# Long-convolution stage: all 16 tap units with two ScalarE products and two partial sums, first output rows and residual addition inside the fixed order, fixed order made anew

## Chip, cores, metric

The kernel runs on one core of a Trainium2 chip. The metric is the device time of one execution in microseconds. Times inside the profile are counted from the start of the profiled execution's span. The engines are TensorE (PE; PEld is its weight load), VectorE (DVE), ScalarE (ACT), GpSimd (POOL) and SyncE (SP), which issues most DMAs. Each engine runs its own instructions in order; between engines they wait on semaphores.

## What is computed

One adaLN block on S = 2048 rows of D = 448 channels, float32, batch 1. Cut to what matters:

```python
sa, ca, ga, sb, cb, gb = (silu(c) @ w_mod) in six pieces of D
h  = layernorm(x) * (1 + ca) + sa                   # x = A_q
# conv branch: short causal conv of K, times V, long causal conv, gate
k_shift = sum(k_pad[:, t:t + S, :] * shift_k[:, 3 - t] for t in range(4))
kv = k_shift * v
y  = irfft(rfft(kv, 2 * S) * rfft(ssm_k, 2 * S))[:S] + kv * ssm_D
x  = x + ga * (h * y)
# gated MLP, F = 1792
h  = layernorm(x) * (1 + cb) + sb
x  = x + gb * ((sigmoid(h @ w_gate) * (h @ w_up)) @ w_down)
```

## The kernel before, in words

There are two parts. The second, the gated MLP, is a long run of TensorE matmuls from about 169 us to the end. The first is the conv branch, and only this one is changed.

**Conv branch.** The channels are handled in two halves `h` of C = 224, and each half in two groups `c` of DT = 112. The long convolution is done as a discrete Fourier transform in matrix form, in steps, for the filter (`k`, tile `ak`) and for the signal (`v`, tile `av`): `s1k`/`s1v` (TensorE, first transform; four indices `i` with two halves `e` each), `e1k`/`e1v` (ScalarE copies the result from PSUM, L262), `tk`/`tv` (VectorE transposes in place a block `n` of eight, L212), `s2k`/`s2v` (TensorE, second transform, L277 and L329), `ek` (ScalarE copy, L280). Then per block the complex product: `m0` and `m1` (VectorE, L332 and L335; `m1` reads a copy `kx` with exchanged parts, which SP's DMAs make, L249), `sa` (TensorE, back transform, L342), `st` (VectorE transpose from PSUM, L346). When the blocks of a half are done, `stage_out` makes output rows `y` (TensorE, L361) from the transposed blocks; `y` of the second half is split for its first four row tiles into `y10`: the columns of blocks 0 to 6 (196 of 224), and those of block 7 (28).

**Taps.** The short convolution works on k stored with the channels on partitions: a unit is (h, i, c), 16 in all, each 112x512. A unit has four taps `t0` to `t3`: a product (`product`, L295 ScalarE or L297 GpSimd) writes into one of six accumulators, and `add_tap` (VectorE, L302, a fused multiply-add) adds a tap to a partial sum: its last argument says which. Tap 3 is written in place over the k tile. Units of half 0 have one product (GpSimd) and three additions into one sum; units of half 1 have one product on GpSimd and one on ScalarE, and one addition to each, thus two partial sums. `kv` (TensorE, L310) turns a unit by transposes against the identity and adds up the partial sums in PSUM: four matmuls for one sum, eight for two. `vm` (VectorE, L314) multiplies by v.

**Beside it.** The layer norm's sums of a row tile pair `ln` (ScalarE, L440 and L441), square root `sq` (ScalarE, L445), its end `le` (VectorE reciprocal and product, L449 and L450), normalised rows `gn` (ScalarE for half 1, L457; GpSimd for half 0, L459), modulation `gm` (GpSimd, two instructions, L463 and L464), the gate's products and sums `ga` and `gb` (GpSimd). The modulation vectors come from `wm` (load), `part` (TensorE), `pc` (ScalarE), `sum` (TensorE), `sc`. 

**What sets the order.** All of this stands in one table, `ORDER`, a list of items that is run from left to right (`run`). An item `t1.1.0.0.a.4` is tap 1 of unit (1, 0, 0) as a product on ScalarE into accumulator 4 (`p`: GpSimd, `d`: VectorE's addition to the sum numbered last); `kv.0.3.0:1` has behind the colon its PSUM buffer (0 to 3: t0, t1, sa, y). Each engine executes its part of the list in that order and nothing is reordered afterwards. SP's loads, too, are issued in the order of the list. Behind `run(ORDER)` follow, in written code, the first weight forms (`plain_hi`, ScalarE), the two pieces of `y10` (`stage_out`), their gate (VectorE, L618: `gg = gg * y`, both pieces), the addition into `x1` (L621), and the statistics of the second layer norm (`ln2_stats`, L476).

Of the kernel before, what the change touches and what calls it, by code (L numbers as in the profile page):

```python
# [32 lines left out]
kv.0.3.1 s2k.0.0:3 tk.0.3 e1v.0.2.1 wm.1 s2k.0.2:0 vm.0.1 ek.0.0 s1k.1.3.1:3 vm.0.3 ek.0.2 s1v.0.1.1:2 t2.1.1.0.d.0 e1k.1.3.1 da.1 s1v.0.3.0:1 tk.0.4
e1v.0.1.1 t0.1.3.1.p.5 s1v.0.1.0:3 t3.1.1.0.d.1 e1v.0.3.0 t2.1.3.1.d.0 s1v.0.3.1:2 t0.1.2.1.p.4 e1v.0.1.0 tk.0.1 s2k.0.4:1 e1v.0.3.1 t2.1.2.1.d.0
s2k.0.1:3 ek.0.4 tv.0.6 s1k.1.0.0:2 ek.0.1 t2.1.0.1.d.0 s1k.1.2.1:1 e1k.1.0.0 tk.0.5 s2k.0.3:3 e1k.1.2.1 s1k.1.1.0:2 t3.1.0.1.d.1 ek.0.3 tv.0.4
kv.1.0.0:1 t0.1.1.1.p.0 e1k.1.1.0 s2k.0.5:3 tk.0.6 t1.1.1.1.a.3 kv.1.0.1 ek.0.5 t2.1.1.1.d.0 s1k.1.0.1:2 tv.0.2 t1.1.2.1.a.1 s2k.0.6:3 e1k.1.0.1
t3.1.2.1.d.1 s1k.1.3.0:0 t3.1.1.1.d.1 ek.0.6 s1k.1.1.1:2 tv.0.0 e1k.1.3.0 kv.1.1.0:3 tk.0.7 e1k.1.1.1 s1k.1.2.0:0 t1.1.3.1.a.2 tv.0.7 kv.1.1.1
e1k.1.2.0 t3.1.3.1.d.1 s2k.0.7:2 ln.0 vm.1.1 vm.1.0 s1v.1.1.1:3 t0.1.2.0.p.2 s1v.1.1.0:0 tk.1.5 t0.1.3.0.p.0 ek.0.7 s1v.1.0.0:1 t2.1.2.0.d.0
t1.1.2.0.a.3 t2.1.3.0.d.0 s1v.1.0.1:2 e1v.1.1.1 t3.1.2.0.d.1 e1v.1.1.0 part.1:3 tk.1.7 t1.1.3.0.a.3 kv.1.2.0:0 tk.1.1 wm.0 pc.1 e1v.1.0.1 kv.1.2.1
t3.1.3.0.d.1 e1v.1.0.0 tk.1.3 kv.1.3.0:2 ln.1 sum.1 vm.1.2 kv.1.3.1 tk.1.2 s1v.1.2.1:0 kx.0.0:0 vm.1.3 s1v.1.2.0:1 e1v.1.2.1 tk.1.0 s1v.1.3.0:2  # L40
# [71 lines left out]
def adaln_conv_glu_kernel(ctx: ExitStack, tc: tile.TileContext, q, kT, v, ssm, shift, dskip,  # L112
# [503 lines left out]
    for c, y in zip(parts, y10):  # L616
        gg = four(gt[1, 0], c)
        DVE.tensor_mul(gg, gg, y.rearrange("p b (j c) -> p b j c", c=C)[:, :, :, c])  # L618
# [614 lines left out]
```

## Time and profile before

| what | value |
|---|---|
| timed runs, median of 3 | 553.51 us (553.46 to 553.8) |
| profiled execution, its own time | 553.13 us |
| its span, first to last instruction | 551.3 us |
| PE busy | 526.7 us (96%) |
| VectorE busy | 445.9 us (81%) |
| ScalarE busy | 259.1 us (47%) |
| GpSimd busy | 84.5 us (15%) |
| mean granted TensorE clock | 0.99 |

The shares are means over two parts with different limits, so they do not say which engine the conv branch waits for; tables of stretches, waits and single rows do. In rows of the timeline the first number is the start and the second the duration, in us; what stands in square brackets is the idle time of the engine ahead of the row, and who ended it. Successive instructions of an engine overlap a little, so the distance of two starts is what one takes of its queue.

### The profile page before, as it was taken

The numbers are of one execution on the slowest core, as the hardware profiler recorded it, in microseconds if no ns is written. First come the engines' busy times: TensorE is split into PE (matmuls) and PEld (weight loads), VectorE is DVE, ScalarE is ACT, GpSimd is POOL, SyncE is SP. The second block draws the span as 40 slices with busy tenths as digits, with TensorE's granted clock in tenths as the row PEclk, the third lists the DMA queues.
The fourth block names the chain that finished last, engine by engine and source line by source line (L and its number), as shares of the span: only waits on it lengthen the run. The fifth ranks groups of instructions, "written<-read, shape, count | busy, mean of one in ns | idle before, by whom it ended". The sixth has DMA issues, their size and how long they took to land.

```text
span 551.3 us, 7602 instructions
## 1 busy us (share of the span) xinstructions
PE 526.7 (96%) x2886; PEld 414.6 (75%) x2886; DVE 445.9 (81%) x551; ACT 259.1 (47%) x444; POOL 84.5 (15%) x64
## 2 busy tenths in 40 slices
PE   3799999999799999999999999999999999999997
PEld 3676733343578888888888888888888888888886
DVE  4999999998898878898998988884646466969565
ACT  1389999821676585375455543421212122424120
POOL 5742216999200000000000000000000000000000
PEclk9799999999899999999999999999999999999999
DMA  8995487872030429486966394767464661220103
GB/s 304 391 410 213 123 247 191 239 200 60 1 111 0 168 92 347 158 324 223 355 243 256 125 360 139 264 229 251 126 210 124 219 226 62 85 98 15 53 0 134
DMA packets 28600, 101.66 MB, mean 184 GB/s; under 512 B 4242, under 2 KB 4756, under 8 KB 27540
## 3 DMA queue, kind: packets, MB, share of 16 engines
q1 hardware_dynamic: 21828, 76.12, 42.1%
q10 hardware_dynamic: 6736, 25.06, 11.6%
q8 instruction: 23, 0.38, 0.3%
q14 instruction: 13, 0.11, 0.1%
HBM read 64.86 MB, written 28.44 MB: 169 GB/s over the span
## 4 chain that ended last, share of the span: by engine, by line
PE 75%; DVE 10%; ACT 5%; DMA 4%; issue 3%; SPq 2%; POOL 0%; DVEq 0%; ACTq 0%
PE d L793 24%; PE b L759 16%; PE c L759 10%; PE a L759 10%; PE gu L881 5%; PE s1k L257 2%; DMA kTa<-in_wmod_dram 2%; SPq L249 1%; PE sa L342 1%; PE kv L310 1%; PE y L361 1%; PE s1v L257 1%; DVE spare L302 1%; PE s2k L277 1%; ACT gbrow L441 1%
## 5 line engine op out<-in xcount | busy, mean ns | idle before, releaser
L793 PE MATMUL d<-wd,h 128*128 128x448 f32 x666 | 144.4, 366 | 0.2
L793 PEld LDWEIGHTS d<-wd,h 128*128 128x128 f32 x666 | 124.7, 188 | 13.1 <-DVE wd L513 1.0
L759 PE MATMUL b<-xt,ring 128*128 128x512 f32 x408 | 99.0, 391 | 0.0
L759 PEld LDWEIGHTS b<-xt,ring 128*128 128x128 f32 x408 | 76.5, 188 | 14.9 <-ACT wd L509 0.2
L808 DVE TENSOR_TENSOR x<-x,d 128x896 f32<-128x896 f32 x55 | 59.5, 1083 | 16.6 <-PE d L793 16.5
L759 PE MATMUL a<-x,ring 128*128 128x512 f32 x264 | 63.8, 389 | 0.0
L759 PEld LDWEIGHTS a<-x,ring 128*128 128x128 f32 x264 | 49.6, 188 | 10.2
L768 ACT ACTIVATE h<-st 128x512 fp32r<-128x512 f32 x55 | 34.6, 629 | 31.4 <-DVE st L777 19.0
L771 DVE TENSOR_TENSOR h<-st,h 128x512 fp32r<-128x512 f32 x55 | 37.8, 688 | 12.5 <-ACT h L768 12.2
L774 ACT ACTIVATE st<-st 128x512 f32<-128x512 f32 x24 | 15.2, 632 | 63.8 <-DVE st L1117 36.0
L881 PE MATMUL gu<-x,ring 128*128 128x512 f32 x176 | 42.7, 397 | 0.0
L1071 ACT ACTIVATE st<-st 128x512 f32<-128x512 f32 x12 | 7.6, 631 | 68.0 <-DVE st L1070 68.0
L881 PEld LDWEIGHTS gu<-x,ring 128*128 128x128 f32 x176 | 33.4, 192 | 7.0 <-DVE inb L922 0.3
L759 PE MATMUL c<-x,ring 128*128 128x512 f32 x144 | 34.8, 390 | 0.0
L740 ACT ACTIVATE ring<-sum 128x512 fp32r<-128x512 f32 x28 | 17.2, 625 | 31.7 <-DVE sum L721 16.8
L759 PEld LDWEIGHTS c<-x,ring 128*128 128x128 f32 x144 | 27.0, 188 | 5.2
L342 PE MATMUL sa<-m,wa 128*64 128x448 f32 x128 | 27.1, 548 | 2.4 <-DVE m L335 2.4
L759 PE MATMUL c<-xt,ring 128*128 128x512 f32 x120 | 29.2, 389 | 0.0
L777 DVE TENSOR_TENSOR st<-st 128x512 f32<-128x512 f32 x24 | 16.6, 691 | 11.9 <-ACT st L774 11.7
L759 PEld LDWEIGHTS c<-xt,ring 128*128 128x128 f32 x120 | 22.5, 188 | 4.6
L342 PEld LDWEIGHTS sa<-m,wa 128*64 128x64 f32 x128 | 8.4, 136 | 20.1 <-issue 12.1
L262 ACT ACTIVATE ak<-s1k 128x896 f32<-128x896 f32 x16 | 14.4, 920 | 19.0 <-PE s1k L257 19.0
(189 smaller groups left out, 830.1 us busy)
## 6 DMA issues: line engine op xcount, KB each, us to landing
fd<-ring ACTq DMA_DIRECT2D x35, 512.0 KB, 5.2
...
```

The costliest lines, as they stand in the source:

```text
L257: PE.matmul(y, zc[r, g + jj], xs_[r, jj], start=True, stop=True)
L262: ACT.activation(d, y, AF.Copy)
L342: PE.matmul(wide[r, b, :, :56], wa[:, b, r], pairs2(ms[:, k])[:, b], start=True, stop=True)
L740: ACT.activation(forms[name, i][:, 0], w_src(name), AF.Copy)
L759: PE.matmul(pt, wh(s, t), x[:, k], start=start and m == 0, stop=stop and m == len(ops) - 1, skip_group_check=True)
L768: ACT.activation(hh, h, AF.Copy)
L771: DVE.tensor_sub(hl, h, hh)
L774: ACT.activation(y[:, 0], y[:, 0], AF.Sigmoid)
L777: DVE.tensor_mul(y[:, 0], y[:, 0], y[:, 1])
L793: PE.matmul(y, h[:, (2 * e + i) * P:(2 * e + i + 1) * P], x, start=m == 0, stop=m == len(ops) - 1)
L808: DVE.tensor_add(y, y, rows(pt))
L881: PE.matmul(pt[:, g], plain(q, t)[:, s, g, f * P:f * P + P], xf[xs_[b]][:, k], start=m == 0, stop=m == 10, skip_group_check=True)
```

## The change

1. Every unit gets two products on ScalarE (taps 0 and 1) and two partial sums (taps 2 and 3 each one VectorE addition). GpSimd's 16 products go, ScalarE's become 32 instead of 8, VectorE's additions 32 instead of 40, and the transposes of the eight units of half 0 double from 32 to 64.
2. The two pieces of `y10`, the gate and the addition are items of the list (`y10`, `gma`, `gaa`). The gate's product is now written into the PSUM buffer of `y` instead of over `gt`, and the addition reads it there.
3. The whole list is in another order, with other accumulators and PSUM buffers.

```diff
 ORDER = """
-kt.0.0.0 kt.0.1.0 ssm.0.2 kt.0.1.1 kt.0.1.2 v.0.3 zc.3 kt.0.0.1 zc.2 kt.0.0.3 v.0.0 dr.1 dr.0 t0.0.0.1.p.0 ssm.0.0 kt.0.0.2 t0.0.0.0.p.1 t1.0.0.1.d.0
...
-y.0.3:2 gm.0.2 st.1.7 st.1.6 part.5:3 yc.3 pc.5 sum.5 ga.2 sc.5 ga.3
+kt.0.0.0 zc.3 ssm.0.3 kt.0.1.0 kt.1.1.0 kt.0.1.1 kt.0.0.1 kt.0.0.2 dr.1 t1.0.0.0.a.0 ssm.0.1 zc.1 t0.0.0.0.a.1 zc.2 t2.0.0.0.d.0 kt.0.1.3 s1k.0.3.1:0
...
+pc.5 m0.1.7:2 ga.2 m1.1.7:3 sum.5 st.1.6 sa.1.7:3 sc.5 gm.0.1 y10.0:1 st.1.7 y10.1:3 gma.0 gma.1 gaa.0 ga.1 gaa.1 gb.1
 """
...
+    parts = slice(0, 7 * 28), slice(7 * 28, C)
+
+    def do_y10(e, pt):
+        stage_out(1, 0, None, parts[e], pt)
+
+    def do_gma(e, pt):
+        g, y = [x.rearrange("p b (j c) -> p b j c", c=C)[:, :, :, parts[e]] for x in (pairs(gt[1, 0]), rows(pt))]
+        DVE.tensor_mul(y, g, y)
+
+    def do_gaa(e, pt):
+        c = parts[e]
+        x = x1[:, 0:4, C + c.start:C + c.stop].rearrange("p (b j) c -> p b j c", b=2)
+        DVE.tensor_add(x, x, rows(pt).rearrange("p b (j c) -> p b j c", c=C)[:, :, :, c])
...
-    parts = slice(0, 7 * 28), slice(7 * 28, C)
-    y10 = [stage_out(1, 0, "t", parts[0])]
-    y10.append(stage_out(1, 0, "t", parts[1]))
-    four = lambda x, c: pairs(x).rearrange("p b (j c) -> p b j c", c=C)[:, :, :, c]
-    for c, y in zip(parts, y10):
-        gg = four(gt[1, 0], c)
-        DVE.tensor_mul(gg, gg, y.rearrange("p b (j c) -> p b j c", c=C)[:, :, :, c])
-    for c in parts:
-        xs_ = x1[:, 0:4, C + c.start:C + c.stop]
-        DVE.tensor_add(xs_, xs_, gt[1, 0][:, :, c])
```

What the new list does to single engines, at three places. First ScalarE, from its sigmoid at the start of the program: before, its first instructions are copies of `s1k` results (L262), with products (L295, here for half 1) in between:

```order
L548 ACTIVATE cols<-cv 112x4
L262 ACTIVATE ak_81<-s1k_2_1_185 128x2x8x56
L262 ACTIVATE ak_81<-s1k_2_0_194 128x2x8x56
L262 ACTIVATE ak_81<-s1k_0_1_217 128x2x8x56
L262 ACTIVATE ak_81<-s1k_0_0_231 128x2x8x56
L295 ACTIVATE m<-kTb,sk 112x512
L262 ACTIVATE ak_81<-s1k_1_0_242 128x2x8x56
```

and in the changed kernel, from the same sigmoid:

```order
L562 ACTIVATE cols<-cv 112x4
L295 ACTIVATE spare<-kTa,sk 112x512 x2
L262 ACTIVATE ak_81<-s1k_3_1_151 128x2x8x56
L262 ACTIVATE ak_81<-s1k_3_0_159 128x2x8x56
L295 ACTIVATE spare<-kTa,sk 112x512 x2
L295 ACTIVATE spare<-m,sk 112x512
L295 ACTIVATE m<-m,sk 112x512
L295 ACTIVATE m<-kTa,sk 112x512
L295 ACTIVATE spare<-kTa,sk 112x512 x2
```

Products (into accumulators in `spare` and `m`) now stand from the first instruction on, and the copies between them. Second VectorE, around the end of the first layer norm, where it waits for ScalarE's square root; before, with the last transposes of L212 and the first product of L332 ahead of it:

```order
L212 STREAM_TRANSPOSE av_79<-av_79 128x28x16x2
L332 TENSOR_TENSOR m<-s2v_0_668,ak_81 128x896
L449 RECIPROCAL rstd<-rstd 128x4
L450 TENSOR_TENSOR nmr<-nmr,rstd 128x4
L335 TENSOR_TENSOR m<-s2v_0_668,kTb 128x896
L212 STREAM_TRANSPOSE av_79<-av_79 128x28x16x2
```

and in the changed kernel, from the same first product of L332 on:

```order
L332 TENSOR_TENSOR m<-s2v_0_693,ak_81 128x896
L335 TENSOR_TENSOR m<-s2v_0_693,kTb 128x896
L212 STREAM_TRANSPOSE av_83<-av_83 128x28x16x2
L332 TENSOR_TENSOR m<-s2v_1_717,ak_81 128x896
L335 TENSOR_TENSOR m<-s2v_1_717,kTb 128x896
L332 TENSOR_TENSOR m<-s2v_2_737,ak_81 128x896
L335 TENSOR_TENSOR m<-s2v_2_737,kTb 128x896
L346 STREAM_TRANSPOSE av_79<-sa_0_725 128x28x16x2
L463 RECIPROCAL rstd<-rstd 128x4
L464 TENSOR_TENSOR nmr<-nmr,rstd 128x4
```

The reciprocal stands seven instructions further behind the first product (and one transpose of L212 more stands ahead of that product). Third TensorE at the end of the stage; before, from the last `sa` (back transform of block 7, half 1) through `y` of half 0 and the modulation sum (`part`) to `y10` (here `y_0_1192` and `y_0_1201`):

```order
L342 MATMUL sa_7_1152<-m,wa 64x8x56 x4
L361 MATMUL y_3_1158<-av_79,spare 64x224 x8
L409 MATMUL part_1171<-kTa,scb 32x224 x8
L417 MATMUL part_1171<-kTa,ones 128x448
L361 MATMUL y_0_1192<-av_83,spare 64x196 x8
L361 MATMUL y_0_1201<-av_83,spare 64x28 x8
```

and in the changed kernel:

```order
L423 MATMUL part_1186<-kTa,scb 32x224 x8
L342 MATMUL sa_6_1196<-m,wa 64x8x56 x4
L431 MATMUL part_1186<-kTa,ones 128x448
L342 MATMUL sa_7_1207<-m,wa 64x8x56 x4
L361 MATMUL y_0_1215<-av_83,spare 64x196 x8
L361 MATMUL y_1_1225<-av_83,spare 64x28 x8
```

The modulation sum moved ahead of the last `sa`, `y` of half 0 far ahead of it, and `y10` (`y_0_1215` and `y_1_1225`) follows the last `sa` at once.

More of the change, by code (lines that the diff above doesn't have):

```diff
@@ L33 @@
[L33 to L40, printed above, removed]
@@ L45 @@
-s2k.1.3:3 st.0.3 kx.0.7:1 sa.0.4:2 m0.0.5:1 ek.1.3 m1.0.5:3 part.4:0 ln.4 st.0.4 kx.1.0:2 s2v.0.6:1 gm.0.0 sa.0.5:3 tv.1.1 wm.3 m0.0.6:2 pc.4
-s2v.0.7:2 ln.7 st.0.5 sum.4 m1.0.6:1 gm.1.1 s2k.1.5:3 m0.0.7:3 kx.1.1:0 s2v.1.0:1 sc.4 ek.1.5 m1.0.7:0 sa.0.6:0 sq.3 ln.5 le.3 kx.1.2:1 tmp tv.1.3
-sa.0.7:2 st.0.6 gn.0.3 gu.2.4 m0.1.0:2 part.3:3 gu.0.2 gn.1.3 s2v.1.1:0 gm.1.0 st.0.7 wm.5 m1.1.0:3 y.0.0:2 pc.3 sq.2 m0.1.1:0 kx.1.3:2 sa.1.0:1 le.2
-yc.0 m1.1.1:1 gn.1.2 ga.0 tv.1.4 kx.1.4:0 sa.1.1:0 st.1.0 s2v.1.2:2 gb.0 st.1.1 sum.3 m0.1.2:0 y.0.1:0 sc.3 gm.0.3 m1.1.2:1 tv.1.5 kx.1.5:1 s2v.1.3:2
@@ new lines @@
+kv.1.1.1 tv.0.5 t0.1.3.0.a.0 s1v.1.0.0:2 t1.1.2.0.a.2 t2.1.3.1.d.0 s1v.1.0.1:0 t0.1.2.0.a.3 vm.1.1 t1.1.3.0.a.4 t2.1.2.0.d.0 part.1:3 e1k.1.1.0
+t2.1.3.0.d.0 e1v.1.0.1 s1v.1.1.1:1 wm.0 t3.1.2.0.d.1 pc.1 t3.1.3.0.d.1 kv.1.2.0:0 t1.1.3.1.a.2 tk.1.7 sum.1 e1v.1.1.1 t3.1.3.1.d.1 e1v.1.0.0
+s1v.1.1.0:1 tk.1.2 sc.1 kv.1.3.0:2 e1v.1.1.0 tk.1.6 kv.1.2.1 ln.0 tk.1.4 kv.1.3.1 part.0:1 vm.1.3 kx.0.0:0 s2k.1.4:3 vm.1.2 pc.0 s1v.1.3.1:2 ek.1.4
+tk.1.3 s1v.1.3.0:0 kx.0.1:1 e1v.1.3.1 tk.1.1 s1v.1.2.1:3 e1v.1.3.0 tk.1.5 s1v.1.2.0:2 e1v.1.2.1 s2v.0.0:0 tk.1.0 kx.0.2:2 e1v.1.2.0 sum.0 ln.3
@@ new lines @@
+gn.0.3 st.0.5 s2v.0.7:2 sc.4 sq.1 gn.1.3 s2k.1.5:3 le.1 gm.0.3 m1.0.6:0 part.3:0 m0.0.7:1 kx.1.1:0 sa.0.6:1 pc.3 gn.1.1 m1.0.7:3 sum.3 st.0.6 tmp
+gu.2.4 ek.1.5 gm.1.3 s2v.1.0:2 gu.0.2 tv.1.4 kx.1.2:1 sc.3 ln.4 sa.0.7:3 m0.1.0:2 m1.1.0:0 s2v.1.1:0 wm.5 st.0.7 sa.1.0:2 ln.5 kx.1.3:2 gn.0.1
+m0.1.1:1 y.0.1:3 st.1.0 gm.1.1 m1.1.1:2 y.0.0:2 sq.2 yc.1 le.2 kx.1.4:0 tv.1.5 gn.1.2 s2v.1.2:3 tv.1.7 sa.1.1:0 m0.1.2:0 yc.0 gn.0.2 m1.1.2:3 y.0.3:2
+st.1.1 kx.1.5:1 ga.0 s2v.1.3:3 tv.1.6 yc.3 sa.1.2:0 m0.1.3:1 ga.3 m1.1.3:2 s2v.1.4:2 st.1.2 sa.1.3:3 kx.1.6:2 gm.1.2 m0.1.4:0 s2v.1.5:0 m1.1.4:1
@@ L52 @@
+y.0.2:1 st.1.3 kx.1.7:0 m0.1.5:2 sa.1.4:3 yc.2 gb.0 m1.1.5:3 s2v.1.6:1 st.1.4 gm.0.2 sa.1.5:0 m0.1.6:0 s2v.1.7:3 m1.1.6:1 part.5:2 st.1.5 sa.1.6:1
+pc.5 m0.1.7:2 ga.2 m1.1.7:3 sum.5 st.1.6 sa.1.7:3 sc.5 gm.0.1 y10.0:1 st.1.7 y10.1:3 gma.0 gma.1 gaa.0 ga.1 gaa.1 gb.1
 """
```

35 lines of the change are left out of this document (19 added, 16 removed).

## Prediction

> **What bounds the kernel now.** First the table of stretches, cut where the work changes: for each stretch the busy time and count of PE, PEld, DVE, ACT and POOL, then the granted clock, the DMA share and GB/s.
>
> ```profile
> 8.15:72.98 64.83, 55.32 (x468) 39.77 (x468) 62.46 (x71) 46.90 (x69) 27.65 (x17) 0.95 0.77 282
> 72.98:135.15 62.17, 58.88 (x464) 22.11 (x462) 61.43 (x68) 37.20 (x86) 47.88 (x35) 1.00 0.71 197
> 135.15:142.53 7.38, 5.94 (x70) 3.90 (x63) 3.67 (x4) 3.66 (x7) 6.23 (x3) 1.00 0.01 3
> 142.53:168.80 26.27, 22.88 (x116) 17.81 (x112) 23.66 (x45) 20.78 (x37) 0.00 (x0) 0.94 0.18 58
> 168.80:551.30 382.50, 379.02 (x1763) 326.66 (x1763) 293.82 (x359) 149.09 (x246) 0.00 (x0) 1.00 0.50 176
> ```
>
> From 168.8 us on PE is busy for 379.0 of 382.5 us; the change leaves that part as it is, and it simply starts earlier or later. The convolution before it, up to 142.53 us, is VectorE's: 62.46 of 64.83 us, then 61.43 of 62.17. So what counts is how early VectorE ends the last addition into x1 (142.53 us), after which its rows are the old ones. Second view, who VectorE waits for from its first tap (8.15 us) to there, longest first; all others together are under 2.5 us:
>
> ```profile
> DVE inb L618 <- PE y L361: 3.7, 1, 3.7
> ```
>
> One wait matters, at the very end; the rest is work. Hence two questions: how much VectorE work goes, and whether the engines that take it over can still feed VectorE.
>
> **Term 1, VectorE's work.** Eight units lose one fused multiply-add each (the tap that ScalarE now multiplies); 40 such additions become 32. Their groups in the first 60 us (count, then busy us and mean ns of one):
>
> ```profile
> L302 DVE SCALAR_TENSOR_TENSOR spare<-kTa,sk,spare 112x512 f32<-112x512 f32 x16 | 14.3, 929 | 7.4 <-DMA kTa<-in_kT_dram 6.2 <-POOL spare L297 1.1
> L302 DVE SCALAR_TENSOR_TENSOR kTa<-kTa,sk,spare 112x512 f32<-112x512 f32 x8 | 6.3, 812 | 0.1
> L302 DVE SCALAR_TENSOR_TENSOR m<-m,sk,spare 112x512 f32<-112x512 f32 x4 | 2.9, 740 | 0.2 <-ACT spare L295 0.2
> ```
>
> Four additions late in the stage take 2.9 us, 0.725 each; the 16 that run while GpSimd multiplies take 14.3, 0.89 each, and the 8 after them 0.79. I read the excess as the two engines disturbing each other, which goes with GpSimd's 16 products: 16 x 0.17 + 8 x 0.06 = 3.2 us. Removed work is 8 x 0.725 = 5.8. Together VectorE could lead by **9.0 us**.
>
> **Term 2, ScalarE's bill.** All 32 products are ScalarE's now, 24 more than before. A product and its successor, the sums of two row tiles up to what follows them, a small copy, then three stretches (ScalarE is the fourth busy time; they are cut at the end of its first sigmoid, at its fourth L262, at its first and its last square root), and the first square root with the VectorE instruction that waits for it:
>
> ```profile
> 59.90 0.71 ACT L295 ACTIVATE spare<-kTb,sk 112x512 f32<-112x512 f32 x1
> 60.51 1.71 ACT L262 ACTIVATE av<-s1v 128x896 f32<-128x896 f32 x2
> 56.24 0.57 ACT L440 ACTIVATE gbrow<-x 128x448 f32<-128x448 f32 x1
> 59.10 0.90 ACT L280 ACTIVATE ak<-s2k 128x896 f32<-128x896 f32 x1
> 71.30 0.57 ACT L434 ACTIVATE arow<-part 128x448 f32<-128x448 f32 x1
> ...
> 5.93:25.30 19.37, 9.30 (x49) 6.96 (x48) 15.91 (x18) 2.75 (x3) 15.20 (x11) 0.90 1.02 377
> 25.30:74.00 48.70, 47.72 (x432) 33.56 (x436) 47.58 (x55) 45.15 (x66) 14.54 (x10) 0.97 0.69 246
> 74.00:106.40 32.40, 30.82 (x252) 10.39 (x244) 31.93 (x38) 30.47 (x75) 19.72 (x19) 1.00 0.80 227
> ...
> 74.00 0.30 ACT L445 ACTIVATE rstd<-rstd,cols 128x4 f32<-128x4 f32 x1
> 74.33 0.18 DVE L449 RECIPROCAL rstd<-rstd 128x4 f32<-128x4 f32 x1 [0.31 <-ACT rstd L445]
> ```
>
> A product takes 0.61 us of the queue (59.90 to 60.51): 24 are 14.6 us. ScalarE is nearly idle until 25.3 us (2.75 of 19.37 busy) and nearly full after it, so the products must go into that early hole. The checkpoint is the first square root, 74.00, for which VectorE already waits now (0.31 us, in the brackets). In the new order there stand in front of it, besides the 24 products, two more copies of L280 (0.8 each, as half of the 1.71 us pair), the sums of two more row tiles (56.24 to 59.10, 2.9) and one more L434 (0.5 with the overlap): 19.6 us more in all. Idle until 74.0 is 16.6 + 3.6 = 20.2 us. Without any idle the square root comes at 73.4; the full stretch now idles 3.6 of 48.7 us with its queue never short of work, and I take that share again: 77.3, and VectorE's reciprocal 77.6.
>
> VectorE's lead there: the new order has eight more 1.0 us instructions in front of that reciprocal (two transposes of L212, five products with m, one transpose of L346), and eight additions fewer. Same work done would be 74.33 + 8.1 = 82.4, so the lead is 82.4 - 77.6 = **4.8 us**, not 9.0: VectorE waits about 4 us there. From there to the last root ScalarE has 30.47 - 5.1 = 25.4 us of work and VectorE 26 of its 1.0 us instructions and some small ones, some 28, so the lead is kept.
>
> **Term 3, the end of the stage.** These rows are VectorE, PE and GpSimd from the last product on:
>
> ```profile
> 130.04 1.08 DVE L335 TENSOR_TENSOR m<-s2v,kTb 128x896 f32<-128x896 f32 x1
> 131.04 4.11 DVE L346 STREAM_TRANSPOSE av<-sa 128x896 f32<-128x896 f32 x4
> 131.27 1.72 PE L342 MATMUL sa<-m,wa 128*64 128x448 f32 x8 [0.36 <-DVE m L335]
> 132.79 1.78 PE L361 MATMUL y<-av,spare 128*64 128x224 f32 x16
> 136.19 1.02 PE L417 MATMUL part<-kTa,ones 128*128 128x448 f32 x2 [0.72 <-ACT kTa L412]
> 137.14 2.04 PE L361 MATMUL y<-av,spare 128*64 128x196 f32 x32
> 138.87 1.15 DVE L618 TENSOR_TENSOR inb<-inb,y 128x784 f32<-128x784 f32 x2 [3.72 <-PE y L361]
> 139.93 2.60 DVE L621 TENSOR_TENSOR x<-x,inb 128x784 f32<-128x784 f32 x2
> 137.36 4.15 POOL L397 TENSOR_TENSOR tmp<-tmp,zc 128x896 f32<-128x896 f32 x2
> ```
>
> Now the last product ends at 131.13, and 11.4 us pass to 142.53: PE does y.0.3 and the modulation sum (which waits for ScalarE) before y10, and L621, both operands in SBUF, needs 2.60 us where L618 of the same size needs 1.15. It ends 1.0 us after GpSimd's last instruction (141.51). In the new PE order y.0.3 is far ahead and the sum stands before the last `sa`; `y10.0` needs only blocks 0 to 6 and runs beside the last transpose. After the last product: 0.14 + 1.72 (`sa`), y10.0 1.6, gate 1.15, addition 1.15 (one operand is in PSUM now, as in L618; as much as 2.60 if it is held up as L621), 5.8 with the hand-overs. Two transposes instead of four follow the last product, so two more (2.0) stand ahead of it: gain 11.4 - 2.0 - 5.8 = **3.6 us**. That VectorE writes a product into PSUM is not in this trace; the nearest rows are L618 (1.15 a pair) and L621 (2.60), so it costs 0 to 1.5 us; I take L618, the same product with the same operands, and 0.
>
> **Term 4, GpSimd.** Its products go, but its gate work (L459 on) now runs one tile deeper into the end, and it holds up small VectorE instructions with two SBUF operands:
>
> ```profile
> 86.99 0.16 DVE L450 TENSOR_TENSOR nmr<-nmr,rstd 128x4 f32<-128x4 f32 x1
> 101.61 1.11 DVE L450 TENSOR_TENSOR nmr<-nmr,rstd 128x4 f32<-128x4 f32 x1
> 100.58 2.11 POOL L464 TENSOR_TENSOR inb<-inb,brow 128x896 f32<-128x896 f32 x1
> ```
>
> The same 4-column product takes 0.16 or, until GpSimd's instruction ends, 1.11. With the three later ones and the statistics behind the stage meeting a busy GpSimd, 0 to 4 us; I take **-1.0**. The gates themselves are not late: GpSimd's chain ends at 141.51 now, starts 5 to 6 us earlier (the lead, and one product fewer ahead of `arow`) and is one tile of L459 longer, so it ends near 138, and its last addition (gb.1) is wanted only by the statistics of tiles 4 to 7, behind those of tiles 0 to 3 and the first gu products. The loads change order, not bytes:
>
> ```profile
> 8.15 3.05 DVE L302 SCALAR_TENSOR_TENSOR spare<-kTa,sk,spare 112x512 f32<-112x512 f32 x3 [6.23 <-DMA kTa<-in_kT_dram]
> 50.00:55.00 5.00, 5.00 (x46) 3.60 (x48) 5.00 (x6) 4.64 (x6) 0.00 (x0) 1.00 0.01 5
> ```
>
> They are all in by 50 us (DMA share 0.01 from there), and the taps of the last k tiles stand near 48 us in the new order: 0, or up to +2 where a tap waits; I take 0.
>
> **Sum.** 4.8 + 3.6 - 1.0 = 7.4 us; 553.13 (profiled execution; its span is 551.3) - 7.4 = 545.7. The median of the timed runs is 553.51, 0.4 above it: I forecast 546.0.
>
> **Rivals.**
> (a) ScalarE keeps up, the whole 9.0 passes: 553.5 - 9.0 - 3.6 = 541. Against it: ScalarE may then not idle at all after 8 us; I give it 0.13.
> (b) The lead is eaten, only the end remains: 553.5 - 3.6 = 550. PE is the other candidate: eight units with two parts to turn instead of one cost
>
> ```profile
> 33.90 0.53 PE kv L310 x4
> 47.18 0.92 PE kv L310 x8
> 26.20 1.79 PE s1k L257 x8
> 31.43 0.96 PE s1k L257 x8
> 13.72 1.73 PE L310 MATMUL kv<-ident,kTa 112*128 112x112 f32 x8 [7.11 <-issue]
> 10.00:15.00 5.00, 1.28 (x7) 1.31 (x8) 4.60 (x6) 0.00 (x0) 4.58 (x3) 1.00 1.01 380
> 20.00:25.00 5.00, 2.93 (x18) 1.92 (x14) 4.23 (x5) 0.92 (x1) 4.91 (x3) 0.66 1.03 406
> ```
>
> 8 x 0.39 = 3.1 us, most of it early where PE has room; but from 22 to 55 us the chain runs along PE too. And the clock: in the stretch granted 0.66 and just behind it the same group of PE takes 1.79 us instead of 0.96. If some 5 to 8 us of that state fall where PE has become the feeder, 2 to 4 us of the lead go. The Trainium skill (TensorE: Matmul & The Clock Gate, Part 1) says that the array is throttled to half after an idle window of about 3.4 us and is released only by sustained work. This trace agrees only in part: PE idled for 7.1 us before 13.72, and yet the clock was full from 10 to 15 us and fell only in the stretch from 20. By the rule a PE with gaps between 8 and 16 us runs cold there and the sum is 548 to 550; by the row it stays 546. Chance of (b) 0.18.
> (c) No change that can be measured, 552.4 to 554.6: the lead is lost as in (b) and the two-operand waits take the end's 3.6 as well: 0.06.
> (d) **Slower**: the early hole is not filled. If the new order of loads leaves ScalarE's products waiting, its bill moves behind everything. The last square root is at 106.40 now, with the same ScalarE work ahead of it but for the 14.6 us of products. From it to 142.53 are 36.1 us; the new order leaves three 1.0 us instructions fewer behind it and saves term 3, which makes 29.5. So the kernel gets slower when that root comes after 113, that is when ScalarE puts less than 8 of the 14.6 us into its idle time (106.4 + 14.6 - 8.0 = 113). With 6 the root is at 115 and the kernel at 555.5. For it: the products wait in one queue, in order, behind copies that wait for PE and loads. Against it: the hole is 16.6 us wide and the first addition of a tap starts at 8.15 us already now. 0.08.
>
> **How the numbers follow.** Forecast 546.0 (its own range 543.5 to 548.5) 0.55, (a) 0.13, (b) 0.18, (c) 0.06, (d) 0.08. Faster by over 0.2% (1.1 us, about what can be told from no change here): 0.86; same 0.06; slower 0.08. The range reaches to (a) and (b): 541.0 to 551.0, which leaves out (c) and (d) and a little of (a).
>
> **What would show it.** ScalarE busy over 11 of the 19.4 us up to 25 us (else d); additions of L302 all near 0.73 (else term 1); VectorE's reciprocal at 77.6 with a wait of some us on ScalarE (at 73 to 74: a; a wait on PE kv or s1k in front of it instead: b); 5.8 us from the last product to the last addition and no SBUF pair there (term 3). Wrong altogether if the part from 168.8 on takes other than 382.5 us.

## The result, and the profile after

| what | before | changed kernel |
|---|---|---|
| timed runs, median | 553.52 us (553.46 to 553.8) | 546.83 us (545.92 to 547.66) |
| profiled execution, its own time | 553.13 us | 547.66 us |
| its span | 551.3 us | 545.9 us |

The ratio is 0.9878 with a 95% interval of 0.9861 to 0.9895: 6.7 us faster. The profiled execution of the changed kernel is the slowest of its four, so what follows accounts for 5.4 us (551.3 to 545.9); and the four lie 1.7 us apart, where those of before lie 0.3 apart. Both facts come back below.

In the changed kernel's listing the lines after `do_y` stand 14 further down: L463 and L464 are L449 and L450 of before, L459 is the square root; the gate and the addition of the first row tiles are L396 and L401.

The table of stretches, first of before and then of the changed kernel, cut at the same four points of the program: VectorE's first tap, its first reciprocal (end of the layer norm's first four row tiles), the end of its last product L335, the end of the last addition into x1. Columns as in the prediction: the stretch, its length, the busy time and count of PE, PEld, VectorE, ScalarE and GpSimd, then clock, DMA share and GB/s.

```profile
8.15:74.33 66.18, 56.67 (x480) 40.28 (x484) 63.50 (x72) 48.20 (x70) 27.65 (x17) 0.95 0.77 279
74.33:131.13 56.80, 53.64 (x414) 19.23 (x406) 56.37 (x63) 35.36 (x83) 43.97 (x31) 1.00 0.77 213
131.13:142.53 11.40, 9.83 (x102) 6.26 (x103) 7.68 (x8) 4.20 (x7) 10.14 (x8) 1.00 0.01 2
142.53:551.30 408.77, 401.90 (x1878) 344.47 (x1874) 317.49 (x403) 169.86 (x282) 0.00 (x0) 0.99 0.48 168
```

```profile
8.59:79.89 71.30, 68.81 (x568) 45.50 (x572) 63.44 (x72) 66.34 (x103) 1.43 (x2) 1.00 0.85 305
79.89:130.22 50.33, 48.87 (x395) 18.45 (x388) 49.52 (x57) 32.11 (x74) 44.85 (x34) 1.00 0.68 184
130.22:136.55 6.33, 6.04 (x60) 3.32 (x61) 4.41 (x7) 2.62 (x5) 6.17 (x4) 1.00 0.01 3
136.55:545.90 409.35, 403.06 (x1886) 345.02 (x1886) 317.65 (x403) 170.16 (x282) 3.11 (x2) 1.00 0.48 168
```

The gain is the sum of four differences, once the moved instructions are counted where they now stand (8.1 us of VectorE's work went from the second stretch into the first, 2.0 us from the third into the second):

- up to the reciprocal: 66.18 + 8.1 - 71.30 - 0.44 (the first tap is later by 8.59 - 8.15) = **2.5 us**
- from there to the last product: 56.80 - 8.1 + 2.0 - 50.33 = **0.4 us**
- the end of the stage: 11.40 - 2.0 - 6.33 = **3.1 us**
- the rest of the program: 408.77 - 409.35 = **-0.6 us**

In the first stretch VectorE has 8.2 us less to do (63.50 + 8.1 - 63.44), but it now idles 7.86 us there instead of 2.68: five of the eight saved microseconds became waiting. ScalarE is busy for 66.34 of 71.30 us. The view of VectorE's waits from its first tap to 150 us, longest first (whom, us in total, times, longest; the row with 10.8 contains the 6.7 us ahead of the first tap):

```profile
DVE spare L302 <- ACT spare L295: 10.8, 5, 6.7
DVE av L346 <- PE sa L342: 1.7, 2, 1.5
DVE rstd L463 <- ACT rstd L459: 1.2, 1, 1.2
```

Where it waits first: ScalarE and VectorE at the start, in order of time (in brackets the idle time ahead of the row and who ended it).

```profile
7.13 0.21 ACT L562 ACTIVATE cols<-cv 112x4 f32<-112x4 f32 x1 [3.23 <-DMA cv<-in_cvec_dram]
8.42 3.36 PE L257 MATMUL s1k<-inb,zc 64*128 64x224 f32 x16 [1.80 <-DMA inb<-in_ssm_dram]
10.32 0.92 ACT L262 ACTIVATE ak<-s1k 128x896 f32<-128x896 f32 x1 [1.76 <-PE s1k L257]
11.82 0.92 ACT L262 ACTIVATE ak<-s1k 128x896 f32<-128x896 f32 x1 [0.57 <-PE s1k L257]
12.63 1.32 ACT L295 ACTIVATE spare<-kTa,sk 112x512 f32<-112x512 f32 x2
13.38 0.75 DVE L302 SCALAR_TENSOR_TENSOR spare<-kTa,sk,spare 112x512 f32<-112x512 f32 x1 [3.25 <-ACT spare L295]
```

The third and fourth product (12.63) stand in ScalarE's queue behind two copies that wait for TensorE's first s1k. VectorE, which before took its products from GpSimd, now waits 3.25 us for TensorE by way of ScalarE.

The end of the stage, the rows that answer to those of term 3:

```profile
129.15 1.07 DVE L335 TENSOR_TENSOR m<-s2v,kTb 128x896 f32<-128x896 f32 x1
131.01 1.72 PE L342 MATMUL sa<-m,wa 128*64 128x448 f32 x8
132.56 3.66 PE L361 MATMUL y<-av,spare 128*64 128x196 f32 x48
132.78 1.12 DVE L346 STREAM_TRANSPOSE av<-sa 128x896 f32<-128x896 f32 x1 [1.49 <-PE sa L342]
134.33 1.16 DVE L396 TENSOR_TENSOR y<-inb,y 128x784 f32<-128x784 f32 x2 [0.43 <-PE y L361]
135.40 1.15 DVE L401 TENSOR_TENSOR x<-x,y 128x784 f32<-128x784 f32 x2
135.48 2.11 POOL L409 TENSOR_TENSOR kTa<-kTa,tmp 128x896 f32<-128x896 f32 x1
```

y10 follows the last sa at once, and the addition takes 1.15 us for the pair, beside a working GpSimd.

### The profile page after: what moved, and what is told of

Same layout as the page of the kernel before. It is cut to its first block, busy times and chain, and to the rows that moved or that the text cites. A ratio compares the mean times of both kernels' runs of the same rounds, so it can differ in the third digit from the quotient of the medians.

```text
span 545.9 us, 7676 instructions
## 1 busy us (share of the span) xinstructions
PE 531.6 (97%) x2918; PEld 416.8 (76%) x2918; DVE 435.9 (80%) x543; ACT 273.9 (50%) x468; POOL 56.8 (10%) x48
## 4 chain that ended last, share of the span: by engine, by line
PE 82%; ACT 7%; DVE 7%; DMA 2%; issue 2%; ACTq 0%; DVEq 0%
PE d L797 24%; PE b L763 16%; PE c L763 10%; PE a L763 10%; PE gu L885 5%; PE sa L342 4%; PE kv L310 2%; PE s2k L277 2%; PE s2v L329 2%; PE s1v L257 2%; PE s1k L257 1%; DMA cv<-in_cvec_dram 1%; DMA kTa<-in_kT_dram 1%; ACT m L295 1%; PE y L361 1%
## 5 line engine op out<-in xcount | busy, mean ns | idle before, releaser
L1052 DVE TENSOR_TENSOR st<-b,st 128x1024 f32<-128x1024 f32 x11 | 13.4, 1222 | 9.0 <-PE b L763 8.9
```

Source lines behind the costliest of these rows:

```text
L1052: DVE.tensor_add(u2, pb_, c1)
```

## The experiments

Twelve kernels. Two theories stood at the start, of the 2.3 us by which the first square root came later than predicted (79.56 instead of 77.3). **A**: ScalarE's total work caps VectorE, as term 2 has it. **B**: VectorE loses its lead in single waits at the start, and ScalarE is only beside it. Further theories came from the first runs: **C** for the stretch from 57 to 95 us, **E** for TensorE's speed.

### pool6: ScalarE relieved of six products

```diff
-t1.1.1.0.a.0 tk.0.1 kv.1.0.1 t0.1.1.0.a.5
+t1.1.1.0.a.0 tk.0.1 kv.1.0.1 t0.1.1.0.p.5
...
```

> The changed kernel, with six of its 32 products (first taps of six units of half 1) back on GpSimd, so that ScalarE has 6 x 0.61 = 3.7 us less to do between 30 and 58 us. Theory A (ScalarE's total work sets when VectorE gets past the first layer norm, as the prediction's term 2 has it): the first square root comes 2.5 to 3.7 us earlier than 79.6, VectorE's reciprocal follows it at 77 or before, the kernel is at 544 to 545.5. Theory B (VectorE's lead is lost already before 25 us, in its waits of 3.25 and 0.44 us for the first products; after 25 us it is full by itself and ScalarE only costs the 1.2 us wait at the reciprocal): the reciprocal moves by at most 1.2 us, to 78.7 or later, additions near GpSimd's products take 0.8 to 0.9 us instead of 0.75, and the kernel stays at 546 to 547.5.

Measured: 548.17 us (548.02 to 548.33), ratio 0.9907 (0.9890 to 0.9923): slower than both theories allow. The stretch 28 to 60 us of the changed kernel, and of pool6:

```profile
28.00:60.00 32.00, 31.60 (x292) 21.26 (x289) 30.65 (x36) 30.18 (x41) 0.00 (x0) 1.00 0.72 280
```

```profile
28.00:60.00 32.00, 31.02 (x284) 20.36 (x280) 29.09 (x34) 26.45 (x34) 10.30 (x7) 1.00 0.73 283
```

and a row each of its VectorE and ScalarE:

```profile
58.40 1.42 DVE L302 SCALAR_TENSOR_TENSOR spare<-kTb,sk,spare 112x512 f32<-112x512 f32 x2 [0.92 <-POOL spare L297]
60.51 0.72 ACT L295 ACTIVATE spare<-m,sk 112x512 f32<-112x512 f32 x1 [1.40 <-DVE kTb L302]
```

ScalarE does its 3.7 us less (26.45 instead of 30.18) and gives them back as idle time, because VectorE now waits for GpSimd's products and ScalarE's next product waits for VectorE. Of the slowing by contention little is seen: the 32 additions' slowest kind has a mean of 845 ns. The reciprocal comes at 81.27, 1.4 us later than in the changed kernel, and its wait is 1.21 us again. Less work on ScalarE gains nothing here, but the run does not decide against A: a product takes 1.56 us on GpSimd, so the run also delays what VectorE waits for. The run ln_short below takes work from ScalarE without that.

### fill and sig: the waits at the start

`fill` moves two products ahead of the two copies that wait for TensorE, `sig` the sigmoid out of their way:

```diff
-... s1k.0.3.0:1 e1k.0.3.1 dr.0 zc.0 e1k.0.3.0 ssm.0.2 kt.0.0.3 t0.0.0.1.a.0 v.0.1 v.0.2 t1.0.0.1.a.2 t2.0.0.1.d.0
+... s1k.0.3.0:1 dr.0 zc.0 ssm.0.2 kt.0.0.3 t1.0.0.1.a.2 v.0.1 v.0.2 t0.0.0.1.a.0 t2.0.0.1.d.0 e1k.0.3.1 e1k.0.3.0
```

> The changed kernel, with ScalarE's third and fourth product (unit 0,0,1) moved ahead of its first two copies of s1k results, whose wait for TensorE (1.76 and 0.57 us of idle ScalarE) they now fill; their k tile lands at about 9.8 us. No work is added or removed. Theory B: VectorE's second tap starts near 11.2 instead of 13.4 us, some 2 us of its wait go, and the reciprocal is reached as much earlier unless ScalarE holds it; kernel at 545 to 546. Theory A: ScalarE's idle time before 13 us shrinks by about 1 us, so the square root comes 1 us earlier, at 78.6, whatever VectorE has; kernel 1 us faster, near 545.8. Third possibility: the copies come late for TensorE's next s1k and the 2 us come back as waits for kv or s1k before 30 us; no change.

> The changed kernel, with the sigmoid moved behind ScalarE's first copies (an activation of a constant loads its table at the start instead). In the changed kernel the first products wait behind the sigmoid for the load of cvec until 7.13 us although the first k tile is there at 4.0. Expected: first product near 4.3, VectorE's first tap near 5.6 instead of 8.6 us. Theory B: VectorE's second tap still waits for the third product, which stands behind the copies, so only 0 to 0.5 us are gained: kernel 546.3 to 546.8. Theory A: ScalarE does 1.3 us of products earlier, and about as much comes out at the square root, 78.3; kernel near 545.6.

Measured: fill 545.94 us (545.53 to 546.28), ratio 0.9866 (0.9851 to 0.9880); sig 546.97 (546.28 to 547.34), ratio 0.9883 (0.9869 to 0.9898). Three rows of fill, one of TensorE and two of VectorE, then one of sig:

```profile
8.60 2.51 PE L257 MATMUL s1k<-inb,zc 64*128 64x224 f32 x16 [2.17 <-DMA inb<-in_ssm_dram]
11.31 0.75 DVE L302 SCALAR_TENSOR_TENSOR spare<-kTa,sk,spare 112x512 f32<-112x512 f32 x1 [1.07 <-ACT spare L295]
78.22 0.18 DVE L463 RECIPROCAL rstd<-rstd 128x4 f32<-128x4 f32 x1 [1.22 <-ACT rstd L459]
```

```profile
14.16 0.75 DVE L302 SCALAR_TENSOR_TENSOR spare<-kTa,sk,spare 112x512 f32<-112x512 f32 x1 [6.82 <-ACT spare L295]
```

In fill the second unit's tap comes at 11.31 instead of 13.38; 1.67 us are left of it at the reciprocal, and 1.7 at the end (span 544.2). That fits B: what VectorE loses before 25 us it loses at the end. In sig the first tap comes 3 us earlier (5.81) and that of the second unit at 14.16 all the same, since it hangs on the copies; nothing is gained, as B said and A did not. But fill is no proof of what its edit is worth: its s1k took 2.51 us instead of 3.36 with the same code ahead of it, gate_sbuf below reaches the reciprocal at 77.85 without this edit, and the interval of fill overlaps that of the changed kernel.

### ln3_late and ln_short: ScalarE ahead of the first square root

Theory C says that from 57 to 95 us ScalarE's own work is the limit, by a small margin. The sums of row tiles 6 and 7 are moved behind the square root that does not need them; in ln_short they and those of tiles 0 to 3 are taken over 64 of the 448 columns instead, so that this kernel computes something else.

```diff
-... s1v.1.2.0:2 e1v.1.2.1 s2v.0.0:0 tk.1.0 kx.0.2:2 e1v.1.2.0 sum.0 ln.3
+... s1v.1.2.0:2 e1v.1.2.1 s2v.0.0:0 tk.1.0 kx.0.2:2 e1v.1.2.0 sum.0
...
-sq.0 le.0 st.0.1 gn.0.0
+sq.0 le.0 ln.3 st.0.1 gn.0.0
```

> The changed kernel, with the sums of row tiles 6 and 7 (2.9 us of ScalarE), which the first square root does not need, moved behind it. Total work of ScalarE stays. Both theories: the square root comes 2.9 us earlier, near 76.7, VectorE's wait of 1.2 us at the reciprocal is gone and the reciprocal stands at 78.7. If VectorE alone sets the rest (both theories say so from there on), 1.2 us reach the end: kernel near 545.6. If ScalarE still caps it later, the wait comes back at a later copy, square root or normalised row, and the kernel stays within 0.4 us of 546.8.

> The changed kernel, with the layer norm's sums of row tiles 0 to 3, 6 and 7 taken over 64 of 448 columns only (the sums themselves are thus changed): 12 instructions of about 0.57 and 0.67 us become about 0.2 and 0.3, so ScalarE has 4.5 to 5 us less to do between 62 and 78 us, and nothing else is touched. Theory C (between 57 and 95 us ScalarE's own work is the limit by a small margin, and the wait of 1.2 us at the reciprocal is what VectorE loses to it): the reciprocal stands at 78.7, no wait of 0.85 us at arow (84.5 us) takes its place as it did where only the order was changed, and 1.2 us reach the end: kernel 545.6. Rival, the prediction's rival (a): VectorE gains more than 1.2 us since ScalarE held it up all along by way of TensorE: kernel 544.5 or less. If neither, the wait turns up elsewhere and the kernel stays at 546.8.

Measured: ln3_late 546.11 us (545.55 to 547.81), ratio 0.9874 (0.9857 to 0.9891); ln_short 545.94 (543.62 to 546.25), ratio 0.9854 (0.9831 to 0.9877). VectorE's rows of ln3_late, then of ln_short (where all lines stand one further down):

```profile
78.26 0.18 DVE L463 RECIPROCAL rstd<-rstd 128x4 f32<-128x4 f32 x1 [0.20 <-ACT rstd L459]
84.47 0.62 DVE L442 TENSOR_TENSOR arow<-arow,part 128x448 f32<-128x448 f32 x1 [0.85 <-PE part L431]
132.34 1.12 DVE L346 STREAM_TRANSPOSE av<-sa 128x896 f32<-128x896 f32 x1 [1.49 <-PE sa L342]
```

```profile
78.34 0.18 DVE L464 RECIPROCAL rstd<-rstd 128x4 f32<-128x4 f32 x1 [0.20 <-ACT rstd L460]
131.24 1.12 DVE L346 STREAM_TRANSPOSE av<-sa 128x896 f32<-128x896 f32 x1 [1.49 <-PE sa L342]
```

From the reciprocal to the last transpose the changed kernel takes 132.78 - 79.89 = 52.89 us, ln3_late 54.08 and ln_short 52.90. Reordering removes the wait at the reciprocal (0.20 left) and has it back at once, 0.85 of it at arow; less work removes it for good, and 1.0 us reaches the end. So C holds ahead of the first reciprocal, with 1.0 us for 1.2: ScalarE is the limit there, but by 1 us only. (The other half microsecond of ln_short's 79.89 - 78.34 is there ahead of that wait; its s1k took 2.72 us.) The medians alone would not show it, since both intervals overlap that of the changed kernel. The 3.8 us that ScalarE saved in ln_short (12 instructions, 0.32 each: 0.57 to 0.25 and 0.67 to 0.35) did not bring more, which speaks against rival (a), and against A in the form that ScalarE's total work sets VectorE's pace.

### fill2_sig: six products ahead, no sigmoid

> The changed kernel, with ScalarE's first six products ahead of its first two copies, and the sigmoid behind those copies (a sigmoid of a constant at the start loads the table). VectorE's early waits then end with the loads alone: first tap near 5.8, second unit near 11.0 (its k tile lands at 9.8), the third without a wait. Theory B (what VectorE loses before 25 us reaches the end one for one): taps up to 25 us come 2.5 to 3.5 us earlier than in the changed kernel, the reciprocal at 76.5 to 77.3, kernel at 543.5 to 544.5. Rival: from some point on TensorE's first transform or its loads are late, and VectorE waits for those in front of its first transposes at 29 us: kernel at 545.5 to 546, as with two products moved.

Measured: 547.00 us (546.34 to 547.22), ratio 0.9880 (0.9865 to 0.9895). The first tap comes at 5.69, the second unit at 11.18, but then:

```profile
15.86 0.72 ACT L295 ACTIVATE spare<-kTa,sk 112x512 f32<-112x512 f32 x1 [0.55 <-PE kv L310]
16.61 0.75 DVE L302 SCALAR_TENSOR_TENSOR kTa<-kTa,sk,spare 112x512 f32<-112x512 f32 x1 [1.14 <-ACT spare L295]
```

TensorE is as slow here as in the changed kernel's profile (s1k 3.36 us). kv starts at 14.09 instead of 12.83, 1.3 us later, because its PSUM buffer is freed by the delayed copies, and the next products wait for kv, which still reads their accumulators. At 26 us the lead is 0.4 us (25.96 against 26.38). A miss: the rival named the right engine, at another place.

### warm14: TensorE's speed at the start

```diff
-    warm("y", "warm", 10)
+    warm("y", "warm", 14)
```

> The changed kernel, with 14 instead of 10 matmuls of the constant ahead of TensorE's first work, so that TensorE is busy up to about 8.3 us, when the first s1k's load lands, instead of idle from 6.6. In the runs so far the first 16 matmuls of s1k took 3.36 us (changed kernel, sig, fill2_sig), 3.31 (pool6), 2.5 to 2.8 (fill, ln3_late, ln_short) or 1.78 (gate_sbuf) with the same code ahead of them, and VectorE's first taps moved by up to 1.5 us with it. Theory E (TensorE's speed at the start differs from run to run, and the changed kernel feels it since ScalarE's products stand behind copies of s1k; busy matmuls settle it): the 16 matmuls take 1.8 to 2.0 us, the second unit's tap starts near 12 us, the runs lie within 0.6 us of each other around 545.3 to 545.9. Rival F (the speed is set by something that four more matmuls don't touch): the durations and the scatter of 545.5 to 547.7 stay. A third outcome: the matmuls run at half speed to the end and s1k begins 0.2 to 0.5 us later; 547 to 547.5.

Measured: 547.54 us (547.15 to 548.26), ratio 0.9893 (0.9875 to 0.9911). In the profile TensorE is fast from the start, and VectorE is 2.2 us ahead of the changed kernel at the reciprocal; then it loses that in two places:

```profile
8.37 1.78 PE L257 MATMUL s1k<-inb,zc 64*128 64x224 f32 x16 [0.30 <-DMA inb<-in_ssm_dram]
77.71 0.18 DVE L463 RECIPROCAL rstd<-rstd 128x4 f32<-128x4 f32 x1 [1.22 <-ACT rstd L459]
97.23 0.59 PE L423 MATMUL part<-kTa,scb 112*32 112x224 f32 x8 [0.94 <-DMA kTa<-in_wmod_dram]
99.52 1.12 DVE L346 STREAM_TRANSPOSE av<-sa 128x896 f32<-128x896 f32 x1 [1.33 <-PE sa L342]
107.94 2.09 POOL L478 TENSOR_TENSOR inb<-inb,brow 128x896 f32<-128x896 f32 x1
107.95 2.10 DVE L464 TENSOR_TENSOR nmr<-nmr,rstd 128x4 f32<-128x4 f32 x1
132.73 1.12 DVE L346 STREAM_TRANSPOSE av<-sa 128x896 f32<-128x896 f32 x1 [1.49 <-PE sa L342]
```

TensorE waits for a load of modulation weights with the sa that VectorE needs behind it in its queue (1.33 us), and the 4-column product of the layer norm starts 0.01 us behind a GpSimd instruction and ends with it, 2.10 us instead of the changed kernel's 1.11. At 132.7 nothing is left (132.73 against 132.78). The two places cost 1.33 - 0.18 = 1.15 us more than in the changed kernel, and 2.10 - 1.11 = 0.99. So E is right in its durations and wrong on the time. Whether an early lead must be lost so, this run does not say; gate_sbuf below has the same lead and keeps it. That the runs are above those of the changed kernel by 0.7 us is not explained by this one profile, whose part behind the stage is longer too (410.0 us for 409.35); the intervals overlap.

### gate_sbuf and before_psum: the gate's product

The first undoes the write into PSUM in the changed kernel, the second makes it alone in the kernel before:

```diff
-        DVE.tensor_mul(y, g, y)
+        DVE.tensor_mul(g, g, y)
...
-        DVE.tensor_add(x, x, rows(pt).rearrange("p b (j c) -> p b j c", c=C)[:, :, :, c])
+        DVE.tensor_add(x, x, gt[1, 0][:, :, c])
```

> The changed kernel, with the gate of the first four row tiles written over gt in SBUF as before, so that the addition has two SBUF operands again; order of all instructions as in the changed kernel. Theory (term 3): GpSimd works until 139.7 us there, so the addition is held up as before, about 2.4 to 2.6 us for 784 columns instead of 0.96; the first statistics start 1.5 us later, and the kernel is 1.2 to 1.5 us slower, 548.0 to 548.3. Rival: the tail's gain came from the order of TensorE alone, and the addition takes 1.0 to 1.2 us with SBUF operands too, since nothing holds it up; kernel 546.8.

> The kernel before, with the gate of the first four row tiles written into the PSUM buffer of y and the addition reading it there, nothing else: one half of the prediction's term 3 alone. Theory: the two additions take 1.15 instead of 2.60 us, and the kernel is at 552.0 to 552.2. Rival: the writes into PSUM cost VectorE as much more as the additions save; 553.4.

Measured: gate_sbuf 549.29 us (547.18 to 549.64), ratio 0.9916 (0.9894 to 0.9937); before_psum 551.81 (551.16 to 552.51), ratio 0.9973 (0.9963 to 0.9982), 1.5 us faster than before. The rows of gate_sbuf, then of before_psum (where they are L619 and L622):

```profile
132.16 1.15 DVE L396 TENSOR_TENSOR inb<-inb,y 128x784 f32<-128x784 f32 x2 [0.34 <-PE y L361]
133.24 3.06 DVE L401 TENSOR_TENSOR x<-x,inb 128x784 f32<-128x784 f32 x2
133.41 2.75 POOL L409 TENSOR_TENSOR kTa<-kTa,tmp 128x896 f32<-128x896 f32 x1
```

```profile
139.14 1.16 DVE L619 TENSOR_TENSOR y<-inb,y 128x784 f32<-128x784 f32 x2 [3.82 <-PE y L361]
140.21 1.15 DVE L622 TENSOR_TENSOR x<-x,y 128x784 f32<-128x784 f32 x2
```

With two SBUF operands the pair takes 3.06 us, with one of them in PSUM 1.15; writing the product into PSUM costs nothing (1.16 against 1.15). Both rivals fall. GpSimd is held up too: its instruction takes 2.75 instead of 2.11. The median of gate_sbuf is 2.5 us above that of the changed kernel where 1.2 to 1.5 were expected and the pair's rows account for 1.9; and the profiled run is 2.1 to 2.5 us faster than its three others.

gate_sbuf also shows something else. Up to the gate its code is that of the changed kernel, but its first s1k took 1.78 us for 3.36, and VectorE's reciprocal and last transpose came at

```profile
77.85 0.18 DVE L463 RECIPROCAL rstd<-rstd 128x4 f32<-128x4 f32 x1 [1.21 <-ACT rstd L459]
130.71 1.12 DVE L346 STREAM_TRANSPOSE av<-sa 128x896 f32<-128x896 f32 x1 [1.48 <-PE sa L342]
```

instead of 79.89 and 132.78. The same order, with TensorE fast at the start, is 2.0 us ahead at the reciprocal and 2.1 at the end of the stage. This is the plainest support for B: what is lost early is lost at the end, and TensorE's speed sets how much that is.

### before_act: the same products on ScalarE, in the kernel before

All 16 `p` in the old list become `a`.

> The kernel before, with its 16 GpSimd products done by ScalarE at the same places of the order; nothing else. Theory (term 1: GpSimd's products and VectorE's additions disturb each other, 3.2 us in all): the 40 additions take 0.75 us on average instead of 0.81, the sixteen dearest 0.75 instead of 0.93. VectorE's waits for products then stand in the copies' queue on ScalarE, so the time itself can come out either way; with these waits small it would be near 551, with 3 to 6 us of new waits 553 to 557. Rival: the dear additions are dear for another reason (loads running at the same time): they stay at 0.9 us with GpSimd idle.

Measured: 552.79 us (551.19 to 553.97), ratio 0.9988 (0.9977 to 1.0000), no difference that can be told. The group of additions in before_act that answers to the first row of term 1 (count, busy us, mean ns, idle time ahead):

```profile
L302 DVE SCALAR_TENSOR_TENSOR spare<-kTa,sk,spare 112x512 f32<-112x512 f32 x16 | 11.4, 746 | 4.8 <-ACT spare L295 4.7
```

The sixteen that took 14.3 us (929 ns) beside GpSimd take 11.4 (746). That is 2.9 of the 3.2 us of contention, on the code of before; the eight of the second row of term 1 take 6.2 for 6.3 and hardly change. The rival, loads that run at the same time, falls: from 8 to 33 us the loads keep the DMA as busy as before (a share of 1.03 for 1.02), and the additions are short all the same.

### best and best2: attempts to use all of it

best: fill, 14 matmuls at the start, the sums of tiles 6 and 7 behind `ln.7`, and the copy of a modulation sum, `sc.4`, behind `sq.1`. best2: fill, those sums behind `sq.3`, `sc.4` as in best, `part.3` behind `sa.0.6`, and the 4-column product as a fused form.

```diff
-        DVE.tensor_mul(m, m, r)
+        DVE.scalar_tensor_tensor(m, m, 1.0, r, op0=OP.mult, op1=OP.mult)
```

> The changed kernel with three edits: the third and fourth product ahead of the first copies (as in fill), 14 matmuls of the constant instead of 10, and the sums of row tiles 6 and 7 behind those of 14 and 15, with the copy of the fourth modulation sum behind the third square root instead of ahead of it, so that neither the first reciprocal nor the second modulation sum waits for them. Expected by theories B, C and E together: reciprocal at 76.3 to 76.8 without a wait over 0.3 us, no new wait at arow or at the later reciprocals, kernel at 543.8 to 544.6. If ScalarE is full up to 108 us and gives the time back at the third reciprocal (its root comes 0.25 us ahead of it in the changed kernel): 545.2 to 545.8.

> The changed kernel with five edits, each on a wait that the runs so far showed: third and fourth product ahead of the first copies (as in fill); the sums of row tiles 6 and 7 behind the second square root (in the run best they held up a copy for which s2v waited 1.71 us); the copy of the fourth modulation sum behind the third square root; the third modulation product (part.3) behind the back transform that VectorE waits for, since its load landed only 0.16 us ahead of it in the changed kernel and late in warm14 and sig (1.33 and 1.08 us of VectorE's wait); and the 4-column product of the layer norm as a multiply with two multiplications (the form of L302) instead of the plain product, which GpSimd holds up (0.16 us alone, 1.11 in the changed kernel, 2.10 in warm14). Expected: reciprocal near 77 us with no wait over 0.3, no wait over 0.5 us on VectorE from there to the last product, all four 4-column products at 0.25 us or less, kernel at 543.3 to 544.8, depending on TensorE's speed up to 20 us. If the product in the new form is held up too: 1 us more. If ScalarE, full up to 108 us, gives the layer norm's time back elsewhere: 545 to 546.

Measured: best 547.44 us (546.65 to 548.38), ratio 0.9894 (0.9878 to 0.9910); best2 547.84 (546.76 to 550.33), ratio 0.9891 (0.9874 to 0.9907). Neither beats the changed kernel. GpSimd and VectorE in best2, at its third 4-column product:

```profile
95.11 2.08 POOL L477 TENSOR_TENSOR zc<-zc,arow 128x896 f32<-128x896 f32 x1
96.83 0.38 DVE L464 SCALAR_TENSOR_TENSOR nmr<-nmr,rstd 128x4 f32<-128x4 f32 x1
```

Both reach the reciprocal near 77 us with a wait of 0.20 (77.09 and 77.62) and lose lead soon after. At the last transpose best keeps 0.9 of its 2.8 us (131.84 against 132.78), and best2, whose profiled run is its slowest, is 3.6 us behind (136.40). In best VectorE waits 1.71 us for s2v at 89.25, since the moved sums hold up a copy that frees s2v's PSUM buffer. In best2 it waits 1.87 us at the third reciprocal (96.62), whose sums now stand behind others, and 2.17 for s2v at 105.33, since TensorE waits 1.76 us for the moved copy `sc.4`, which holds a PSUM buffer, and 0.67 for the copy ahead of the moved part of the third. The fused form of the 4-column product is held up like the plain one: 96.83 + 0.38 = 97.21, where GpSimd's instruction ends (95.11 + 2.08 = 97.19). Of the kernels that compute the same, fill has the lowest median, and it cannot be told from the changed kernel.

## Why the prediction was right, step by step

**Term 1** (up to 9.0 us of VectorE's work): 8.2 us less in the first stretch, sized to within a tenth, and the part that was read out of three group means, GpSimd disturbing the additions, is shown by before_act on the old code: 2.9 us of 3.2 on its sixteen rows.

**Term 2** (4.8 us pass): 2.5 us passed in the changed kernel's profile. ScalarE's work was sized right, 67.36 us busy from 7.24 to the square root where 67.5 were counted, but it came later. Its sigmoid ran at 7.13 instead of 5.72, when cvec landed, 1.4 us; and it idled 5.0 us up to the root (67.36 busy of 72.32) where 77.3 - 73.4 = 3.9 were taken. Some 2.0 of the 2.3 us missing go with TensorE's slow start: in gate_sbuf, the same code up to there, the root comes at 77.52 and the reciprocal at 77.85, where 77.3 and 77.6 were predicted (ScalarE begins as late there, 7.11, but idles 3.2 us). That is near in number only, since the place of the waiting was wrong in either run. The prediction put some 4 us of it at the reciprocal; there were 1.23, and 3.25 stood at 13.38, behind two copies that wait for TensorE (1.21 and 1.83 in gate_sbuf). The "bill", a sum of ScalarE's work that VectorE waits for at one place, was the wrong picture: ln_short took 3.8 us off it and VectorE gained 1.0 by that. VectorE gave up its lead in several hand-overs between three engines; of these the early one behind TensorE and the one at the reciprocal were measured, the others were not.

```profile
7.24:79.56 72.32, 68.64 (x560) 45.49 (x564) 63.44 (x72) 67.36 (x105) 1.92 (x4) 1.00 0.85 308
```

**Term 3** (3.6 us): 3.1. The time behind the last product was 6.3 us for 5.8. That the addition would be free of GpSimd with an operand in PSUM, and that the write into PSUM costs nothing, gate_sbuf and before_psum show: 1.5 us of the term, the price that the rows of L618 and L621 gave. The rest, TensorE's new order, was not run by itself; the rows fit it.

**Term 4** (-1.0): +0.4 in the second stretch and -0.6 behind the last addition, -0.2 in its place. The four 4-column products did not get worse: 1.6 us together in the changed kernel (0.16, 0.16, 0.21 and 1.11), 2.3 before. But the price is a matter of phase, as warm14 shows with 2.10 for the last of them, so the term was a guess that could have held. Of the 0.6 us, 0.4 are lost in the statistics and first transposes behind the addition: VectorE's L375 follows the end of that addition by 27.12 us before (169.65) and by 27.53 in the changed kernel (164.08). From there to the end it is 381.65 and 381.82, so the MLP takes as long as before, and the prediction's last sign of being wrong did not appear.

**Sum.** 2.5 + 0.4 + 3.1 - 0.6 = 5.4 for the 7.4 forecast; the profiled execution was the slowest, and the median came out at 546.83, 0.8 above the forecast 546.0 and inside its own range. There is luck in this closeness: term 2 was 2.3 too high and term 3 0.5, term 4 gave 0.8 of it back, and the median lies another 0.8 below the profiled execution.

**Rivals.** (a) is spoken against by ln_short (1.0 us from 3.8 of ScalarE's work) and by gate_sbuf, whose lead at the reciprocal is 82.4 - 77.8 = 4.6 us, not 9.0, with TensorE fast. (d) needed the early hole unfilled; ScalarE is busy for 15.44 of 19.37 us there. (b) had the right engine: its condition, TensorE running slowly up to about 20 us, came true in the changed kernel's profile, 3.36 us for a group that takes 1.78 in gate_sbuf. Its price, 2 to 4 us of the lead, was right at its lower end: 2.0 at the reciprocal and 2.1 at the last transpose, against gate_sbuf. The time stayed within the forecast's own range nevertheless, since the rest of the lead and the end's gain passed. By the rule of the Trainium skill (TensorE: Matmul & The Clock Gate, Part 1) the prediction's 548 to 550 would have come; the rule named the state rightly, and the time was 546.83.

The prediction held its own trace against that rule, and there it misread it. It went by the granted clock of 1.00 from 10 to 15 us; but of the rows that it shows, the eight transposes of kv took 1.73 us at 13.72 and 0.92 at 47.18. TensorE ran slowly there in the kernel before, too.

Open: whether the 1.7 us between the changed kernel's four runs are TensorE's speed at the start. The profiles of one early code show s1k at 1.78 (gate_sbuf), 2.7 to 2.8 (ln_short, ln3_late) and 3.36 us (changed kernel), with VectorE's second unit at 11.95, 13.25 and 13.15, and 13.38. The four runs of gate_sbuf would fit it: the profiled one, fast at the start, took 547.18 us, the others 549.26 to 549.64. But timed runs leave no profile, and warm14, with s1k at 1.78, did not come out faster.
